# Seven of 32 convolution tasks moved from TensorE to GpSimd and VectorE, plain v spread in row halves, the last output tile in column halves, and a new order of all tasks

## The chip, the cores and the metric

One core of one Trainium2 chip runs one program. The metric is the device time of one execution in microseconds (us). The engines are TensorE (PE; its weight loads are listed as PEld), VectorE (DVE), ScalarE (ACT), GpSimd (POOL) and SyncE (SP), which issues nearly all DMAs.

## What is computed

Eight batches of eight heads of attention with a band mask, 576 positions of 64 features; the first four heads look at the 32 last positions (plain), the other four at every fourth of the last 128 (dilated). The result x is gated: a causal convolution over 5 positions per feature gives the gate, a matrix product the value, and a second product the output.

```python
scores = scale * np.matmul(q, k.transpose(0, 1, 3, 2))
mask_plain = (rel >= 0) & (rel < window)                # window 32
mask_dil = (rel >= 0) & (rel < window * dilation) & (rel % dilation == 0)   # dilation 4
scores = np.where(masks[None, :, :, :], scores, -1000000000.0)
attn = np.exp(scores - np.max(scores, axis=-1, keepdims=True))
attn = attn / (np.sum(attn, axis=-1, keepdims=True) + 1e-09)
attn_out = np.matmul(attn, v)
...
for k in range(K):                                      # K = 5
    gate_pre += conv_w[k][None, None, :] * xp[:, k:k + S, :]
gate = 1.0 / (1.0 + np.exp(-gate_pre))
out = (gate * (x @ w_val)) @ w_out
```

q, k, v are (8, 8, 576, 64), the weights 512x512 and 5x512, the output (8, 576, 512), all float32.

## The kernel before

The kernel is a list of some 820 tasks. A task is a function that emits a few instructions, an engine (or a choice of engines) with a cost, the tasks it depends on, and the buffers (`Ten`) that it uses. Buffers belong to classes with fixed counts (`TUNE["n"]`): `ps2` is three pairs of PSUM banks, `ps1` two single banks, `qk`, `va`, `vb`, `vp` hold loaded inputs, `et` exponentials, `xT` the attention result of a batch with features on the partitions, `gate` the gates, `osb` output tiles. `ORDER` is a written list of task numbers, each with a letter for its engine; `Plan.follow` (from line 550 on) emits them in that order, so each engine's queue is in the order of this list, and SP's DMAs too. A task waits for its dependencies and for the last user of the buffer that it is given. A load also waits until the bytes issued ahead of it are few enough (`ahead`). The planner's costs only choose which buffer of a class a task gets.

Names of tasks, with the batch as first digit:
- `Lq`, `Lk` with `p` or `d`: loads of q and k of the plain or dilated heads; `Lf`, `Lr`, `Lv`: plain v; `La`, `Lb`: dilated v; `Lwv`, `Lwo`: the weights, in buffers of class `va`.
- `Td`, `TKp`, `TQp` (L1071, L977): transposes of q and k, evicted by `Q..`, `K..` on ACT or DVE (L908, L910).
- `Sp`, `Sd` (L1001, L1113): scores; `Ep`, `Ed` (L931): exponentials on ACT; `Mp`, `Md`: masks, by two selects on POOL (L814, L816) or one multiplication on DVE (L942).
- `V1`, `V2` (L912): casts of dilated v on POOL; `H`: a clear of padding rows on POOL (L964).
- `Ap` (L1014), `Ad` (L1127, L1136): products with v; `Np`, `Nd`: normalisation on DVE; `Xp`, `Xd`: transposes into `xT`, evicted by `EXp`, `EXd`.
- `Pv` (L871, L877): for batches 0 and 1 plain v is loaded in whole rows and spread over the partitions by products with a 0/1 matrix `spread`, evicted by `Ev`.
- `C` (L1189): the convolution; `G` (L1199): tanh on ACT; `V` (L1207): the value product; `Y` (L1217): (gate + 1) times value on DVE. The digits are batch, half of the positions (288 each), half of the features.
- `O` (L1234): 36 output tiles of 128 positions; `EO` (L1242 on ACT, L1244 on DVE): their eviction; `ST` (L1248): the store.

The convolution on TensorE multiplies with diagonal matrices: for each of 5 taps, two feature chunks and two row halves one 64x64 matmul over 288 columns, 20 in all, four at a time in the four 64x64 quarters of the array. TensorE works in shapes (`mode`): 128 whole rows, `r64` two row halves, `c64` two column halves, `64` four quarters; neighbouring tasks of different shape change it. A value product depends on its convolution task (`t_c`), though it does not read it.

Of the kernel before, what the change touches and what calls it, by code (L numbers as in the profile page):

```python
# [8 lines left out]
FP32 = mybir.dt.float32  # L9
# [230 lines left out]
 'ahead': 7.06,  # L240
# [49 lines left out]
 'n': {'vf': 4,  # L290
# [4 lines left out]
       'va': 4,  # L295
       'vb': 3,
       'vab': 2,
       'vbb': 2,
       'qTp': 2,
       'kTp': 1,  # L300
       'qTd': 3,
       'kTd': 3,
       'et': 13,
       'xn': 5,
       'gate': 7,
       'osb': 15,
       'avt': 2,
       'xT': 3,
# [4 lines left out]
30s 2g 11d 8d 29s 9d 67s 118s 16a 0g 4a 3g 6d 1d 7d 5g 66s 40p 42p 10d 15g 41a 43a 14g 119s 12g  # L313
36p 38p 39d 37a 17a 55p 48p 68s 44p 49a 56a 59p 45a 69s 74p 31s 60a 46d 75d 76a 77p 32s 127p 79a
125p 126d 78a 95p 91p 33s 128d 131p 96a 57d 84p 156s 129p 85a 80p 130d 92a 155s 70p 50d 132a 93g
157s 86d 81a 13d 61d 137p 133p 34g 82d 72p 134a 97d 71a 35g 47p 158s 73d 51p 138a 121s 18p 52d
144p 122s 62p 145a 120s 58p 148p 63d 163p 149a 208s 53p 19a 164d 87p 165a 20g 83p 98p 64p 88d 166p
65a 23s 21s 94p 54a 161p 150d 207s 99d 168a 124g 167a 180p 135d 162d 184p 181a 173p 89p 123g 245s
174a 159p 139d 185a 146d 186d 244s 151p 160a 90d 147p 100p 152d 136p 140p 24g 101a 169p 218p 141d
170a 220p 106p 219a 171d 22g 102p 107a 175d 114p 103a 221d 153p 293s 292s 176p 115a 182d 172p 216p  # L320
108p 177d 217a 154a 214p 27s 109d 187p 183p 215a 116p 188d 226p 142p 25s 227a 117d 178p 246s 233p
222p 143d 234a 248p 223a 179d 251p 250d 249a 189p 104p 252d 253a 265p 105d 110p 266a 190d 258p
111a 254p 267d 299p 329s 303p 259a 199p 304d 255a 28g 260g 195p 235d 200a 191p 228d 196a 193p 256g
26d 300d 112p 192a 194d 330s 305p 113d 197p 306a 301p 198d 717p 247g 209s 211s 269p 718a 237p 210s
257p 261p 238a 732p 262d 270a 331s 203p 733a 271g 224d 336p 204a 302d 333p 239d 337a 322p 335d
723p 323a 338d 212g 415s 334a 272p 268p 729p 724a 273d 213g 225p 263p 730a 229p 343p 230d 339p
726p 340a 264d 344a 240p 414s 727d 307p 354p 308a 231p 236p 274p 355a 241d 205p 332g 378s 275a
294s 341g 201p 206d 232a 345d 276p 295s 356g 202d 296s 346p 277a 342p 242p 347d 738p 377s 243a
350p 311p 309d 318p 351a 720p 739d 319a 416s 352d 421p 312a 324d 418p 423a 422d 388p 420a 353p
297g 357p 278p 358d 419a 499s 298g 721a 288p 279d 428p 289a 359p 389d 280p 429a 360d 435p 281a  # L330
424p 430g 384p 390p 436a 385d 290p 313d 391a 437g 348p 425a 463s 291d 310p 314p 386p 315d 282p
387a 349d 379s 417g 439p 407p 320d 381s 440a 735p 500s 283d 408a 321p 316p 441d 736a 325p 462s
392p 317a 326d 396p 747p 393a 409d 380s 442p 397a 327p 748d 464s 438p 361p 328a 394d 362a 741p
465s 443d 403p 284p 404a 426d 365p 466s 742d 285a 369p 398d 366a 431p 370a 427p 473p 432d 503p
551s 506p 548s 504a 383g 505d 373p 507a 722s 382g 501s 471p 374a 286p 472d 508a 405d 469p 287d
474a 395p 399p 520p 400d 513p 750p 514a 470d 521a 410p 751d 524p 547s 509p 525a 401p 406p 433p
402a 411d 371p 526g 510a 475p 372d 375p 476a 467g 434a 481p 636s 376d 477p 482a 632s 412p 558p
413d 367p 478a 559a 483d 502g 585s 560p 368d 488p 584s 561a 468g 492p 753p 522d 493a 515g 479d
444p 586s 754a 523p 527p 445d 363p 489a 511g 528d 556p 480p 484p 557a 364d 446p 490d 450p 447a
485d 744p 451a 494d 491p 756p 745a 554p 495p 555a 454p 496d 458p 455a 757d 562p 497p 563a 516p  # L340
758s 486p 498d 634s 512p 459a 588p 725s 517d 591p 589a 759p 593a 487d 550s 587g 456p 592d 752s
746s 518p 457d 633s 460p 519a 670s 637g 760d 549s 743s 590a 762p 755s 461d 553g 573p 763d 598p
594p 595a 780p 599a 596g 669s 529p 452p 781a 574a 448p 600g 453d 749s 530a 564d 768p 449d 765p
769a 770s 609p 766d 566p 605p 764s 567a 771p 740s 782s 606a 641p 767s 772d 535p 610a 607g 635s
539p 536a 611d 531p 642d 540a 552g 575d 543p 532a 568d 577p 643p 578a 671s 537p 544a 579d 761s
608p 644a 612p 538d 533p 613d 645p 601p 597p 646a 777p 602d 778a 565p 639p 569p 534d 640a 673p
570d 676p 674a 783p 675a 677d 678a 576p 571p 784d 580p 731s 572a 662p 734s 581d 679p 728s 614p
680a 774p 719s 663a 785s 681d 672g 658p 615d 683p 638g 541p 684a 659a 685d 582p 545p 542d 583a
775a 660d 647p 690p 546d 648a 603p 786p 691a 604d 661p 787d 788s 692g 694p 651p 695a 792p 664d
652a 696d 665p 620p 666d 616p 621a 649d 628p 617a 653d 624p 793d 795p 625a 794s 629a 686p 682p  # L350
789p 796a 687d 697p 693p 630p 698d 667p 654p 631d 668a 626p 790d 650p 688p 655d 699p 689a 622p
# [51 lines left out]
class Plan:  # L403
# [86 lines left out]
    def emit(self, t, eng):  # L490
        t.ins = t.fn(eng)
# [878 lines left out]
```

## Time and profile before

| What | us |
|---|---|
| median of 3 runs | 167.81 (167.54 to 167.93) |
| the profiled execution | 168.98 |
| its span, first to last instruction | 167.3 |
| TensorE busy in it | 152.9 |
| convolution matmuls (L1189), busy | 23.0 |
| value products (L1207), busy | 35.8 |
| output products (L1234), busy | 34.1 |
| DMA, share of 16 engines over the span | 84.7% |

The profile is one execution. Busy time is the time in which an engine had an instruction under way; matmuls overlap, so a busy TensorE is not one at its peak. Rows of the groups name the line, the engine, the operation, what it writes and reads, the shape, the count, then busy time and mean duration, then idle time before and what ended it. The share of DMA over 100% in a stretch comes from packets that overlap.

### The profile page before, as it was taken

Reading aid. Unit: us, or ns where it says so; the run is one execution under the profiler, and the core shown is the slowest. Engines: PE = TensorE matmul, PEld = TensorE weight load, DVE = VectorE, ACT = ScalarE, POOL = GpSimd, SP = SyncE. Lnnn points to the kernel's source line nnn. Section 1 sums busy time; section 2 is a strip of 40 time slices with the busy share of each in tenths; the row PEclk is TensorE's granted clock in tenths of the full one; section 3 lists DMA queues with packets and bytes.
Section 4 is the critical chain, followed back from the end, with each engine's and each line's share of the span. In section 5 each row is a group of like instructions: output and inputs, shape, how many; then the busy total and the mean of one; then the engine's idle time right before and its main releaser. Section 6 shows DMA issues by size and latency. Waiting matters only on the chain.

```text
span 167.3 us, 6119 instructions
## 1 busy us (share of the span) xinstructions
PE 152.9 (91%) x2602; PEld 112.2 (67%) x2621; DVE 117.7 (70%) x250; ACT 110.1 (66%) x184; POOL 51.4 (31%) x86
## 2 busy tenths in 40 slices
PE   0898889989999999999997999999999999999991
PEld 0556677878776676786674876866687667785740
DVE  6127699989797888868757697784789787870520
ACT  4669567876847767777765885656686886357142
POOL 7802554430373370370030770009240221000000
PEclk9999999999999999999999999999999999999999
DMA  5999949999999999989999998179999902100995
GB/s 174 394 386 249 331 139 330 303 396 353 214 293 292 216 387 275 220 314 326 291 266 206 307 341 131 64 243 362 371 402 261 352 20 84 46 0 30 348 352 215
DMA packets 39442, 42.99 MB, mean 257 GB/s; under 512 B 20339, under 2 KB 27640, under 8 KB 39416
## 3 DMA queue, kind: packets, MB, share of 16 engines
q1 hardware_dynamic: 39376, 42.61, 84.7%
q8 instruction: 20, 0.33, 0.9%
q14 instruction: 6, 0.05, 0.1%
q10 hardware_dynamic: 40, 0.01, 0.0%
HBM read 33.17 MB, written 9.44 MB: 255 GB/s over the span
## 4 chain that ended last, share of the span: by engine, by line
PE 71%; DMA 15%; DVE 4%; SPq 4%; issue 2%; ACT 1%; POOL 0%; DVEq 0%; POOLq 0%
PE pd L1207 19%; PE pu L1234 18%; PE pd L1189 12%; DMA qk<-in_q_dram 8%; DMA vb<-in_v_dram 4%; PE pu L1071 3%; PE pd L1113 3%; PE pd L1014 3%; PE pd L1001 2%; PE pd L977 2%; DMA qk<-in_k_dram 2%; PE pu L1034 2%; PE pd L1127 2%; PE pu L1161 2%; SPq L899 2%
## 5 line engine op out<-in xcount | busy, mean ns | idle before, releaser
L931 ACT ACTIVATE et<-pd 128x576 bf16<-128x576 f32 x64 | 39.1, 652 | 13.8 <-PE pd L1113 6.5
L1207 PE MATMUL pd<-xT,w_val 128*128 128x288 bf16 x256 | 35.8, 286 | 0.3 <-DVE qTp L910 0.3
L1234 PE MATMUL pu<-w_out,ya 128*128 128x512 bf16 x126 | 34.1, 380 | 1.5 <-issue 0.8
L1217 DVE SCALAR_TENSOR_TENSOR ya<-gate,pd 128x576 bf16<-128x576 bf16 x32 | 23.7, 749 | 8.0 <-PE pd L1207 5.7
L1207 PEld LDWEIGHTS <-w_val 128*128 128x128 bf16 x256 | 23.7, 98 | 6.5 <-issue 0.6
L1199 ACT ACTIVATE gate<-pd 128x576 bf16<-128x576 f32 x32 | 20.3, 650 | 8.8 <-PE pd L1189 7.3
L1189 PE MATMUL pd<-xT,conv_diag 64*64 64x288 bf16 x640 | 23.0, 285 | 0.4 <-issue 0.2
L942 DVE TENSOR_TENSOR et<-et,mask_d 128x576 bf16<-128x576 bf16 x32 | 18.4, 586 | 3.1 <-ACT et L931 3.1
L814 POOL TENSOR_SCALAR_AFFINE_SELECT et<-et 128x576 bf16<-128x576 bf16 x15 | 11.6, 775 | 28.8 <-ACT et L931 25.6
L1234 PEld LDWEIGHTS <-ya 128*128 128x128 bf16 x144 | 12.2, 97 | 12.1 <-issue 0.9
L1189 PEld LDWEIGHTS <-conv_diag 64*64 64x64 bf16 x640 | 17.6, 106 | 3.4 <-issue 1.4
L1242 ACT ACTIVATE osb<-pu 128x512 f32<-128x512 f32 x21 | 12.6, 600 | 10.6 <-PE pu L1234 10.5
L1071 PE MATMUL pu<-perm_q,qk 128*128 128x128 bf16 x144 | 13.4, 231 | 5.2 <-DMA qk<-in_k_dram 4.7
L1025 DVE TENSOR_TENSOR xn<-pd,rec 96x768 bf16<-96x768 f32 x16 | 15.3, 954 | 0.7 <-DVE rec L1024 0.2
L908 ACT COPY xT<-pu 128x576 bf16<-128x576 bf16 x19 | 11.9, 644 | 5.7 <-PE pu L1161 2.8
L1071 PEld LDWEIGHTS <-qk 128*128 128x128 bf16 x144 | 9.9, 104 | 7.7 <-DMA qk<-in_k_dram 4.7
L1244 DVE TENSOR_SCALAR osb<-pu 128x512 f32<-128x512 f32 x15 | 10.3, 687 | 6.3 <-PE pu L1234 5.7
L1149 DVE TENSOR_TENSOR xn<-pd,rec 128x640 bf16<-128x640 f32 x16 | 13.2, 824 | 0.5
L912 POOL CAST vab<-va 128x1024 bf16<-128x1024 f32 x8 | 8.8, 1106 | 15.3 <-DMA va<-in_v_dram 15.3
L908 ACT COPY kTd<-pu 128x512 bf16<-128x512 bf16 (+1 forms) x12 | 9.0, 747 | 5.1 <-PE pu L1071 3.9
L816 POOL TENSOR_SCALAR_AFFINE_SELECT et<-et 128x576 bf16<-128x576 bf16 x15 | 11.5, 767 | 1.0
L942 DVE TENSOR_TENSOR et<-et,mask_p 128x576 bf16<-128x576 bf16 x17 | 10.0, 598 | 1.3 <-ACT et L931 1.2
(83 smaller groups left out, 209.1 us busy)
## 6 DMA issues: line engine op xcount, KB each, us to landing
qk<-in_k_dram SPq DMA_DIRECT2D x16, 576.0 KB, 6.8
qk<-in_q_dram SPq DMA_DIRECT2D x16, 576.0 KB, 6.7
out_dram<-osb SPq DMA_DIRECT2D x36, 256.0 KB, 3.5
va<-in_v_dram SPq DMA_DIRECT2D x10, 512.0 KB, 6.8
vp<-in_v_dram SPq DMA_DIRECT2D x6, 768.0 KB, 9.6
vb<-in_v_dram SPq DMA_DIRECT2D x16, 128.0 KB, 6.1
va<-in_moe_w_out_dram SPq DMA_DIRECT2D x6, 128.0 KB, 6.0
va<-in_moe_w_val_dram SPq DMA_DIRECT2D x2, 256.0 KB, 6.3
```

The costliest lines, as they stand in the source:

```text
L908: nc.scalar.copy(out=out_, in_=in_)
L931: nc.scalar.activation(out=view(), in_=ps2[ps.idx][:, :, 0:HW], func=AF.Exp, scale=scale)
L942: nc.vector.tensor_tensor(out=ev, in0=ev, in1=m, op=ALU.mult)
L1025: nc.vector.tensor_tensor(out=xn[xt.idx][0:96].rearrange("p (h j) l d -> p h (j l) d", h=2), in0=a[:, :, :, 0:D], in1=rr[:, :, :, None].to ...
L1071: nc.tensor.transpose(out=ov[:, e], in_=a[:, i * 128:(i + 1) * 128], identity=perm_q[o])
L1149: nc.vector.tensor_tensor(out=xn[xt.idx][:, 0:5].rearrange("p n x d -> p x n d"), in0=a[:, :, :, 0:D], in1=rr[:, :, :, None].to_broadcast( ...
L1189: nc.tensor.matmul(out=ps2[pc.idx][64 * ob:64 * ob + 64, n, 0:HW], lhsT=conv_diag[rb, 2 * cp + n, kk, :], rhs=xT[xt.idx][rb, 2 * cp + n, s ...
L1199: nc.scalar.activation(out=gate[g.idx], in_=ps2[pc.idx][:, :, 0:HW], func=AF.Tanh, scale=0.5)
L1207: nc.tensor.matmul(out=ps2[pv.idx][:, n, 0:HW], lhsT=w_val[:, mc, c * 128:(c + 1) * 128], rhs=xT[xt.idx][:, mc, c0:c0 + HW], start=(mc == ...
L1217: nc.vector.scalar_tensor_tensor(out=ya[yt.idx][:, 2 * cp:2 * cp + 2, t0:t0 + HW], in0=gate[g.idx], scalar=1.0, in1=ps2[pv.idx][:, :, 0:HW ...
L1234: nc.tensor.matmul(out=ps1[po.idx], lhsT=ya[yt.idx][:, c, t0:t0 + 128], rhs=w_out[:, c, :], start=(c == 0), stop=(c == NCH - 1))
L1242: nc.scalar.activation(out=osb[ob.idx], in_=ps1[po.idx], func=AF.Copy, scale=0.5)
```

## The change

1. `POOLED` names seven convolution tasks: second half, first features of batches 1 to 6, and first half, first features of batch 7. They become `Cp`: each tap is a scaling of `xT` by a weight per partition into `tap`, in two chunks of 288, and an addition to `acc` (fp32, two buffers). In the order six run on POOL; batch 2's runs on DVE as one scaling and four multiply-adds per chunk. Their tanh `Gp` reads `acc` in three pieces, since the quarters' exchange of halves is done here. No PSUM pair is used. The weights are copied once more, as fp32 (`conv_wf`).
2. Plain v of batches 0 and 1 is spread in one task `Pv`: blocks 0, 1 and 3, 4 need one half of the loaded rows each and are done in pairs of row halves; 32 matmuls are still issued, 8 of them small.
3. The last output tile is done as two tasks of 256 columns, `O35` and `O36`, each with its eviction and store.
4. Score tasks that stand beside a convolution in TensorE's queue are done in quarters (`keys`, `share`), with twice the matmuls; eleven are.
5. `V` no longer depends on `t_c`. Buffer counts change, `ahead` goes from 7.06 to 8.77, and `ORDER` is another list; most tasks stand at another place in it. POOL's selects of masks go from 15 tasks to 16; a cast of w_out moves from POOL to ACT, and the copies that make `perm_m` and `perm_r` from POOL to DVE.

In the new order the pooled tasks stand in POOL's queue so: `Mp110 Cp110 Mp210 H2`, `H4 Cp310 V14 V24`, `V25 Cp410 Cp510 H6 V26 V16 Mp611`, `V17 Cp610 Cp700`. On DVE: `Qd40 Cp210 Y211 Y201`. TensorE ends with `C710 C701 C711 O29 O28 V711 O27 V700 V701 O30 V710 O32 O31 O34 O33 O36 O35`.

```diff
- 'ahead': 7.06,
+ 'ahead': 8.77,
- 'n': {'vf': 4,
+ 'n': {'vf': 5,
...
-       'va': 4,
+       'va': 3,
-       'vbb': 2,
-       'qTp': 2,
+       'vbb': 5,
+       'qTp': 4,
...
-       'qTd': 3,
-       'kTd': 3,
-       'et': 13,
-       'xn': 5,
+       'qTd': 4,
+       'kTd': 2,
+       'et': 10,
+       'xn': 4,
+       'acc': 2,
-       'osb': 15,
+       'osb': 13,
-       'xT': 3,
+       'xT': 2,
...
+    def share(self, tasks):
+
+        run = []
+        for t in tasks + [None]:
+            if t and (t.form or t.mode == "64"):
+                run.append(t)
+                continue
+            if any(not u.form for u in run):
+                for u in run:
+                    if u.form:
+                        u.mode = u.leaves = "64"
+                        u.count *= 2
+            run = []
...
+    POOLED = [(b, 1, 0) for b in range(1, B - 1)] + [(B - 1, 0, 0)]
...
+    acc = tiles("acc", [128, 2, HW], FP32)
+    tap = consts.tile([128, 2, HW], FP32, name="tap")
...
+            def rows(j, rb, c, stop):
+                x0 = SP0 + R * (24 * j - 8) - c
+                nc.tensor.matmul(out=o[j // 4][:, j % 4], lhsT=spread[rb, x0:x0 + 128],
+                                 rhs=a[rb, :, c * D:(c + 1) * D], start=(c == 0), stop=stop)
+            for j in range(2):
+                for c in range(R):
+                    rows(j, slice(0, 64), c, c == R - 1)
+                    rows(j + 3, slice(64, 128), c, c == R - 1)
+            for j in (2, 5):
+                for c in range(R):
+                    rows(j, slice(0, 128), c, c == R - 1 and j == 2)
...
+    def keys(form):
+
+        parts = [slice(0, 128)] if form == "r64" else [slice(0, 64), slice(64, 128)]
+        return [(k, l) for k in parts for l in range(2)]
...
+                if (b, hf, cp) in POOLED:
+                    pc = Ten("acc")
+
+                def conv_p(eng, cp=cp, pc=pc, c0=c0, xt=xt):
+                    for kk in range(K):
+                        s0 = c0 + kk - (K - 1)
+                        for n in range(2):
+                            o = acc[pc.idx][:, n]
+                            i = xT[xt.idx][:, 2 * cp + n, s0:s0 + HW]
+                            w = conv_wf[:, 2 * cp + n, kk:kk + 1]
+                            if eng == DVE and kk:
+                                nc.vector.scalar_tensor_tensor(out=o, in0=i, scalar=w, in1=o, op0=ALU.mult, op1=ALU.add)
+                                continue
+                            e = nc.vector if eng == DVE else nc.gpsimd
+                            e.tensor_scalar(out=tap[:, n] if kk else o, in0=i, scalar1=w, scalar2=None, op0=ALU.mult)
+                        if eng == POOL and kk:
+                            nc.gpsimd.tensor_tensor(out=acc[pc.idx], in0=acc[pc.idx], in1=tap, op=ALU.add)
+
+                def th_p(eng, pc=pc, g=g):
+                    def go(o, i):
+                        nc.scalar.activation(out=o, in_=i, func=AF.Tanh, scale=0.5)
+                    go(gate[g.idx][:, 0], acc[pc.idx][:, 0])
+                    for hb in range(2):
+                        go(gate[g.idx][64 - 64 * hb:128 - 64 * hb, 1], acc[pc.idx][64 * hb:64 * hb + 64, 1])
...
+                if (b, hf, cp) in POOLED:
+                    t_c = plan.add(f"Cp{b}{hf}{cp}", {POOL: 9.0, DVE: 3.5}, conv_p, deps=dc, tens=[pc, g, xt], prio=p)
+                    t_g = plan.add(f"Gp{b}{hf}{cp}", {ACT: 1.05}, th_p, deps=[t_c], tens=[pc, g], prio=p)
...
-                               deps=[x_done[(b, c)] for c in range(NCH)] + w_ready["val"] + [t_c],
+                               deps=[x_done[(b, c)] for c in range(NCH)] + w_ready["val"],
...
+        for i, n0, n1 in [(i, 0, Dm) for i in range(last)] + [(last, 0, Dm // 2), (last + 1, Dm // 2, Dm)]:
+            t0 = 128 * min(i, last)
```

## The prediction

> **What bounds the kernel now.** I read the page's shares first, then the stretches, the chain that ended last, and the groups of the rows that the change prices.
>
> ```profile
> PE 152.9 (91%) x2602; PEld 112.2 (67%) x2621; DVE 117.7 (70%) x250; ACT 110.1 (66%) x184; POOL 51.4 (31%) x86
> PE 71%; DMA 15%; DVE 4%; SPq 4%; issue 2%; ACT 1%; POOL 0%; DVEq 0%; POOLq 0%
> ```
> ```profile
> 0.00:35.00 35.00, 27.74 (x492) 21.20 (x493) 23.27 (x89) 24.18 (x40) 16.96 (x38) 1.00 0.90 293
> 35.00:64.00 29.00, 28.38 (x510) 21.29 (x515) 24.09 (x40) 19.96 (x34) 11.73 (x17) 1.00 1.08 304
> 122.00:150.00 28.00, 27.68 (x491) 20.95 (x490) 23.16 (x41) 18.38 (x31) 3.50 (x5) 1.00 0.53 163
> ```
> The columns are the stretch, its length, busy us of PE, weight loads, DVE, ACT, POOL, then granted clock, DMA share, GB/s. From 35 us on TensorE is busy 28.4 of 29 and 27.7 of 28 us at full clock: there it sets the time, and POOL has room (3.5 of 28 us near the end). Before 35 us the loads set it, as the chain shows:
>
> ```profile
> 12.17 7.38 DMA vb<-in_v_dram
> ...
> 28.43 6.64 DMA qk<-in_q_dram
> ...
> 42.70 0.74 PE pd L1189 x20
> ...
> 120.28 2.58 PE pd L1189 x80
> ...
> 159.91 3.85 PE pu L1234 x17
> 163.78 0.60 ACT osb L1242
> ```
> (start, us, what.) The head is two DMA landings; a convolution task (20 matmuls of L1189) costs the path 0.74 us alone and 2.58/4 = 0.645 us in a run of four; the end is output matmuls, one eviction and a store.
>
> **The convolutions.** Seven of 32 tasks leave TensorE: 7 x 0.645 = 4.5 us off the path (0.74 each would be 5.2). I take 4.5, since most stood in runs. The order has 114 changes of tile shape between neighbouring tasks where it had 111; a change costs about 0.74 - 0.645 = 0.1 us, so +0.3. Eleven score tasks now take the 64x64 shape with twice the matmuls, 12 or 16 in place of 6 or 8; they save a change and double the issue, and I set both to nothing (bounds -1 to +1 us).
>
> **What a convolution costs where it goes.** Six go to POOL, one (batch 2) to DVE. Each POOL task is 10 scalings of 128x288 and 4 additions of 128x576 in fp32. The trace has neither; the nearest rows:
>
> ```profile
> L912 POOL CAST vab<-va 128x1024 bf16<-128x1024 f32 x8 | 8.8, 1106 | 15.3 <-DMA va<-in_v_dram 15.3
> L912 POOL CAST w_val<-va 128x256 bf16<-128x256 f32 x8 | 3.3, 459 | 2.8 <-DMA va<-in_moe_w_val_dram 2.8
> L1284 POOL TENSOR_TENSOR conv_diag<-ident,conv_w 128x1280 bf16<-128x1280 bf16 x1 | 2.3, 2329 | 2.7 <-ACT conv_w L908 2.7
> ```
> The undisturbed casts take 1.04 us for 1024 elements and 0.40 for 256, so 0.83 ns an element and 0.19 us to start: 0.43 us a scaling. An addition by the conv_diag row: 0.19 + 576 x (2329-190)/1280 ns = 1.15 us. With about 0.07 us at each dependent step (the gap between the two POOL selects of one mask), a task is 10 x 0.43 + 4 x 1.15 + 0.4 = 9.3 us. From below: additions at the casts' rate, 0.67 us, give 7.4. From above: fp32 moves twice the bytes of conv_diag's bf16, so twice its rate, 2.1 us, gives 13.1. I take 9.3, because conv_diag is also an operation on two tensors.
>
> The Trainium skill ("GPSIMD Engine Reference", Elementwise — side-by-side cycle accounting) gives 4497 ns for a two-input fp32 addition of 2048 elements; scaled, that estimates 1.26 us here and 9.7 us a task, 0.4 above mine. No run yet shows it.
>
> Beside that comes contention, seen in these lines (start, us, engine):
> ```profile
> 96.88 0.45 DVE L942 TENSOR_TENSOR et<-et,mask_d 128x576 bf16<-128x576 bf16 x1
> ```
> ```profile
> 96.97 0.93 POOL L816 TENSOR_SCALAR_AFFINE_SELECT et<-et 128x576 bf16<-128x576 bf16 x1
> 97.85 0.70 POOL L814 TENSOR_SCALAR_AFFINE_SELECT et<-et 128x576 bf16<-128x576 bf16 x1
> ```
> ```profile
> 98.07 0.79 DVE L942 TENSOR_TENSOR et<-et,mask_p 128x576 bf16<-128x576 bf16 x1
> ```
> The mask multiplication takes 0.45 us; the select that starts during it takes 0.93 in place of 0.71, and the multiplication that starts during the next select takes 0.79. The 49 multiplications range from 441 to 1286 ns. One waits for the other. With 48 multiplications in about 150 us some three meet each 9.3 us task, adding up to 3 x 0.45 = 1.3 us to it.
>
> The Trainium skill ("SBUF — State Buffer", SBUF: two separate sides) says the two engines' common port pair is an exclusive lock held for a whole instruction; the lines agree (0.79 against 0.45 us), and the rule speaks against putting fp32 work on POOL beside these masks.
>
> **Whether POOL keeps up.** I laid out the changed order of TensorE tasks by the mean distance in the trace between one task's first weight load and the next's (convolution 0.70, value product 0.99, output 0.79, scores 0.22 and 0.27 us, and so on), and POOL's queue beside it, at a round 9.0 us a convolution. Behind the convolutions wait clears, casts and masks that TensorE needs. Spare time: 0.7 us at Ap200 (clear H2 behind Cp110), 1.5 at Ad400 (cast V14 behind Cp310), 1.4 at Ap611 (mask behind Cp510). The last two tasks, Cp610 and Cp700, stand back to back after the cast V17 at 131.2; output O32 at 152.9 needs Cp700's tanh and product (1.2 + 0.75 us, and latency) and so the convolution by 150.8: twice its length may be 19.6 us. At 10.6 us for the masked ones and 9.3 for the last, the stalls are 0.9 + 0.1 + 0.2 + 0.3 = 1.5; at 9.3 about 0.3. I take 0.7 (bounds 0 to the slower rival's).
>
> **The DVE task** is 2 scalings and 8 multiply-adds of 128x288. The mask row's 445 ns (576 in two-byte form) bounds one from near: 2 x 0.3 + 8 x 0.445 = 4.2 us; half that if it starts cheaply. It holds DVE between a query eviction and the products Y211, Y201, which free PSUM pairs; three pairs exist. By the layout TensorE needs the first back about 1.9 us before DVE can give it at worst, and other work covers most: +0.5 (0 to 4.2). The seven tanhs are split in three (ACT takes 650 ns for 576 elements and 600 for 512, so 0.2 + 288 x 0.78 ns = 0.42 us each): about 1.2 us for 0.65, on an engine that is 66% busy: nothing on the path. But each waits in ACT's queue for POOL with evictions behind it: Gp410 ahead of a key eviction of batch 6 (transposes done at 102.4, Cp410 at 101.3 to 102.6) and Gp610 ahead of the last xT evictions (141.4, Cp610 at 140.5 to 141.8). At 10.6 us that is 0.4 us at most, and TensorE has value products to do meanwhile, so 0; each us beyond would show.
>
> **Plain v, buffers, tail.** A spread now has 8 pairs of half-row products and 8 whole ones in place of 24. The first task's 16 whole products take 1.76 us from its first weight load to the next task's, 0.11 each, so 8 fewer save 0.9 us a batch, 1.8 in all. Both lie before 35 us, where the landings above decide; I take 0 (bounds -1.8 to +2). The loss bound is from three weight buffers `va` for four: the load of w_val waits for a POOL cast, and the query load whose landing ends at 35.07 stands behind it on SP. Later loads land 1.8 us (q of dilated batch 4, at 70.0) or more ahead of their first use; by then two convolutions, 1.3 us, are saved, so this stays covered, but only just. In the tail half an eviction goes (0.60 us to about 0.4): -0.2, with one store more on SP, 0.43 us, issued while TensorE runs.
>
> **Sum:** -4.5 + 0.3 + 0.7 + 0.5 - 0.2 = -3.2 us. The profiled execution took 168.98 us: 167.3 of span and 1.7 around it; it becomes 165.8, the span 164.1. It lies 1.2 over the median of the runs, so the forecast is 167.8 - 3.2 = 164.6 us.
>
> **Rivals.**
> - *Everything hides* (17%): no stalls, and the head shortens by 1.8. -4.5 - 1.8 + 0.3 - 0.2 = -6.2: 161.6. For: TensorE is busy 27.7 of the first 35 us; against: the two landings.
> - *DVE is the new wait* (16%): Cp210 holds the PSUM pairs back 1.9 us rather than 0.5, and the normalisation Nd30 queued behind it (0.22 + 0.82 us) comes as a second wait of 1.0. -3.2 + 1.4 + 1.0 = -0.8: 167.0. For: 18 of 32 dilated masks met POOL already; against: the longer waits of TensorE on DVE after 35 us are two, 1.2 and 0.3 us.
> - *Slower: POOL cannot keep up* (17%). If a convolution takes 11.5 us (additions at 1.7), the stalls are 1.8 + 1.0 + 1.1, and 2 x 11.5 - 19.6 = 3.4 at the end: 7.3 for my 0.7. 164.6 + 6.6 = 171.2. It decides from 10.8 us a task, where the stalls (1.1 + 0.3 + 0.4 + 2.0) reach the 3.9 that the rest saves. For: fp32, two inputs, the waits on masks; against: conv_diag's row, and that masks are over by about 140 us, so that the last task runs clear.
> - *Gain and stall cancel within 0.2%* (8%), about 10.7 us a task: 167.8.
>
> **How the numbers follow.** The forecast has 42%; its own range is 162.8 to 166.3. Faster by over 0.2% (what these runs can tell from no change): 42 + 17 + 16 = 75%; same 8%; slower 17%. From 161.4, below the best case, to 167.9 all but the slower case is held.
>
> **What would show it.** L1189 at 500 matmuls and near 18 us busy; POOL near 105 us busy, each convolution 9 to 10.6 us from its first scaling to its last addition; scalings near 0.43, additions near 1.15 us; mask multiplications longer on average than 0.53 us; no wait of TensorE over 1 us on POOL; the last POOL addition at least 3 us ahead of O32. Additions near 2 us, or a hole in TensorE before O32, would make the forecast wrong; so would a later first value product than 35.5 us.

## The result and the profile after

The changed kernel takes 212.12 us (median of 4 runs, 211.33 to 213.93) where the kernel before takes 167.68: ratio 1.267 (95% interval 1.258 to 1.275). The forecast was 164.6, in a range of 161.4 to 167.9. The profiled execution took 213.93 us, its span is 212.2, against 167.3 before. In some experiments below (e6, e14 and e15 most) disturbed runs were left out of the ratio but not out of the median, so the text gives differences of medians and, where the two tell otherwise, differences of the ratios beside them.

The page's first parts for the changed kernel, busy time of the engines, the slices of TensorE, GpSimd and the granted clock, and the chain that ended last:

```profile
PE 167.2 (79%) x2557; PEld 116.1 (55%) x2557; DVE 128.5 (61%) x263; ACT 113.8 (54%) x197; POOL 146.1 (69%) x168
...
PE   1788779999809998939969999299479998089383
...
POOL 8205917559996332799957799999933999999700
PEclk9999975899995999985997999969999999658969
...
POOL 50%; PE 29%; DVE 6%; ACT 5%; issue 4%; DMA 3%; POOLq 1%; SPq 0%; DVEq 0%; ACTq 0%
```

GpSimd went from 51.4 to 146.1 us of work and from 0% to 50% of the chain. TensorE is no longer full after 35 us: holes (0, 2, 3, 4) stand where GpSimd shows a run of nines or has just ended one, and after each hole but one (the 4) the granted clock drops. (The 3 near 92 us is a wait for VectorE, which comes below with e6.) Groups of GpSimd, and TensorE's convolutions, on the page (busy us, mean ns of one, idle before):

```profile
L1229 POOL TENSOR_SCALAR tap<-xT,conv_wf 128x288 f32<-128x288 bf16 x48 | 50.2, 1056 | 1.8
...
L1231 POOL TENSOR_TENSOR acc<-acc,tap 128x576 f32<-128x576 f32 x24 | 34.8, 1452 | 2.0
...
L1247 PE MATMUL pd<-xT,conv_diag 64*64 64x288 bf16 x500 | 20.6, 307 | 7.1 <-ACT xT L934 6.8
```

A scaling takes 1.06 us where the prediction had 0.43, an addition 1.45 where it had 1.15. The timeline of GpSimd shows one whole task and what stands behind it (start us, us, and the instruction):

```profile
46.03 1.00 POOL L1229 TENSOR_SCALAR acc<-xT,conv_wf 128x288 f32<-128x288 bf16 x1 [1.94 <-DVE xT L936]
47.01 1.99 POOL L1229 TENSOR_SCALAR tap<-xT,conv_wf 128x288 f32<-128x288 bf16 x2
49.08 1.41 POOL L1231 TENSOR_TENSOR acc<-acc,tap 128x576 f32<-128x576 f32 x1
...
60.85 1.40 POOL L1231 TENSOR_TENSOR acc<-acc,tap 128x576 f32<-128x576 f32 x1
62.20 0.72 POOL L836 TENSOR_SCALAR_AFFINE_SELECT et<-et 128x576 bf16<-128x576 bf16 x1
62.98 0.71 POOL L838 TENSOR_SCALAR_AFFINE_SELECT et<-et 128x576 bf16<-128x576 bf16 x1
63.63 0.31 POOL L995 MEMSET vp<- 32x260 f32 x1
```

The task Cp110 runs from 43.1 to 62.3 (its second scaling, the first row above, waits 1.9 us for an xT eviction), and the clear of `vp` (H2), which the prediction named as first to be late, starts at 63.6. TensorE's timeline at the same place, and the stretches on either side (length, then busy us of PE, weight loads, DVE, ACT, POOL, granted clock, DMA share, GB/s):

```profile
63.99 0.82 PE L1046 MATMUL pd<-vp,et 128*128 128x65 bf16 x12 [6.38 <-POOL vp L995]
```
```profile
56.06:59.47 3.41, 1.55 (x36) 0.85 (x27) 2.40 (x3) 2.31 (x4) 3.23 (x4) 1.00 1.20 257
59.48:62.89 3.41, 0.00 (x0) 0.00 (x0) 0.00 (x0) 0.00 (x0) 3.33 (x4) 1.00 1.21 286
62.90:69.70 6.80, 5.71 (x71) 3.78 (x71) 2.70 (x4) 1.27 (x3) 3.89 (x7) 0.50 0.86 301
```

From 59.48 to 62.89 GpSimd is the only engine that works: everything waits for one clear of 0.3 us that is queued behind a convolution and a mask. Then TensorE runs two windows of 3.41 us at half clock. The view of waits, TensorE's own, shows the same trouble under other names:

```profile
PE pd L1046 <- POOL vp L995: 9.0, 2, 6.4
PE pd L1247 <- ACT xT L934: 6.8, 1, 6.8
...
PE pu L1297 <- DVE ya L1279: 4.1, 1, 4.1
```

(total us, times, longest.) The second and third do not name GpSimd, but lead to it: ScalarE's tanh waits for GpSimd's sum (20.7 us in all, by the view of every engine's waits), and the xT eviction and the product behind the tanh are late with it. That view's row of the tanh, and TensorE's timeline at the longest of these gaps:

```profile
ACT gate L1235 <- POOL acc L1231: 20.7, 4, 7.9
```
```profile
186.63 2.61 PE L1247 MATMUL pd<-xT,conv_diag 64*64 64x288 bf16 x40 [6.81 <-ACT xT L934]
```

TensorE has nine gaps of over a microsecond after 20 us, 31.7 us together, where the kernel before has one, of 1.17 us.

### The profile page after: what moved, and what is told of

It is laid out like the page before. It is cut to its first block, busy times and chain, and to the rows that moved or that the text cites. A ratio compares the mean times of both kernels' runs of the same rounds, so it can differ in the third digit from the quotient of the medians.

```text
span 212.2 us, 6125 instructions
## 1 busy us (share of the span) xinstructions
PE 167.2 (79%) x2557; PEld 116.1 (55%) x2557; DVE 128.5 (61%) x263; ACT 113.8 (54%) x197; POOL 146.1 (69%) x168
## 4 chain that ended last, share of the span: by engine, by line
POOL 50%; PE 29%; DVE 6%; ACT 5%; issue 4%; DMA 3%; POOLq 1%; SPq 0%; DVEq 0%; ACTq 0%
POOL tap L1229 24%; POOL acc L1231 15%; PE pu L1297 6%; POOL acc L1229 5%; PE pd L1269 4%; DMA qk<-in_k_dram 3%; PE pu L1103 3%; PE pd L1008 2%; DVE et L973 2%; PE pd L1247 2%; ACT et L962 2%; POOL vab L938 2%; POOL et L836 2%; POOL et L838 2%; PE pd L1046 2%
## 5 line engine op out<-in xcount | busy, mean ns | idle before, releaser
L1229 POOL TENSOR_SCALAR tap<-xT,conv_wf 128x288 f32<-128x288 bf16 x48 | 50.2, 1056 | 1.8
L1297 PE MATMUL pu<-w_out,ya 128*128 128x512 bf16 (+1 forms) x148 | 42.8, 424 | 4.2 <-DVE ya L1279 4.1
L1231 POOL TENSOR_TENSOR acc<-acc,tap 128x576 f32<-128x576 f32 x24 | 34.8, 1452 | 2.0
L836 POOL TENSOR_SCALAR_AFFINE_SELECT et<-et 128x576 bf16<-128x576 bf16 x16 | 11.7, 734 | 24.4 <-ACT et L962 24.4
L1297 PEld LDWEIGHTS <-ya 128*128 128x128 bf16 x148 | 13.8, 106 | 19.4 <-issue 7.0
L1235 ACT ACTIVATE gate<-acc 64x288 bf16<-64x288 f32 (+1 forms) x21 | 9.3, 441 | 20.9 <-POOL acc L1231 20.7
L1305 ACT ACTIVATE osb<-pu 128x512 f32<-128x512 f32 (+1 forms) x25 | 14.2, 580 | 10.4 <-PE pu L1297 10.2
L1255 ACT ACTIVATE gate<-pd 128x576 bf16<-128x576 f32 x25 | 15.8, 652 | 5.6 <-PE pd L1247 5.5
L1229 POOL TENSOR_SCALAR acc<-xT,conv_wf 128x288 f32<-128x288 bf16 x12 | 12.4, 1042 | 6.5 <-ACT xT L934 4.6
L1046 PEld LDWEIGHTS <-et 128*128 128x128 bf16 x192 | 8.5, 104 | 13.3 <-issue 10.2
L1046 PE MATMUL pd<-vp,et 128*128 128x65 bf16 x144 | 7.3, 206 | 10.4 <-POOL vp L995 9.0
```

Source lines behind the costliest of these rows:

```text
L836: nc.gpsimd.affine_select(out=dst, in_=dst, compare_op=ALU.is_ge, fill=0.0, base=base, pattern=pattern, channel_multiplier=-1)
L1046: nc.tensor.matmul(out=ps2[po.idx][:, hf, (2 * j + l) * DA:(2 * j + l + 1) * DA], lhsT=ex(e, l, 96 * j, 128), rhs=vv[:, 2 * l + x, 3 * hf ...
L1229: e.tensor_scalar(out=tap[:, n] if kk else o, in0=i, scalar1=w, scalar2=None, op0=ALU.mult)
L1231: nc.gpsimd.tensor_tensor(out=acc[pc.idx], in0=acc[pc.idx], in1=tap, op=ALU.add)
L1255: nc.scalar.activation(out=gate[g.idx], in_=ps2[pc.idx][:, :, 0:HW], func=AF.Tanh, scale=0.5)
L1297: nc.tensor.matmul(out=ps1[po.idx][:, 0:n1 - n0], lhsT=ya[yt.idx][:, c, t0:t0 + 128], rhs=w_out[:, c, n0:n1], start=(c == 0), stop=(c == N ...
```

## The experiments

Seventeen kernels, in four groups. Behind each expectation stand the kernel's median and its ratio to the kernel before, run on the same chip, with the 95% interval.

### How long GpSimd's convolution is

**e1: three taps of five.** `for kk in range(K if eng == DVE else 3):` in the convolution; two taps are left out on GpSimd.

> The changed kernel, but the six convolutions on GpSimd compute only the last-but... first three of their five taps (the other two are left out); nothing else is touched. By the rows of the changed kernel's profile such a task takes 2 x 1.00 + 2 x (2.0 + 1.5) = 9.1 us, which is the length that the prediction had priced (9.3). Theory A (the length of a convolution on GpSimd is the one mis-sized term): the rest of the sum holds and the time is about the forecast, 163 to 167 us. Theory B (the new order and the smaller buffers are slow in themselves, whatever GpSimd does): still over 175 us.

176.2 us, ratio 1.054 (1.045 to 1.063). A task takes 9.7 us from first to last instruction (median), and 36 of the 44 lost microseconds are gone. But theory A is out: with a task of about the length that was forecast the kernel is still 8.5 us slower than the one before.

**e2: one tap of five.** The same line with 1 for 3; four taps left out.

> The changed kernel with only the first of five taps on GpSimd (four taps are left out): 2.0 us a task, so that nothing can wait for GpSimd. Theory A: every stall on GpSimd is gone; 162 to 165 us, a little below the three-tap kernel. Theory B: no better than 168 us, because what is left is the order itself.

174.65 us, ratio 1.043 (1.035 to 1.051), at 2.3 us a task. So 7.4 us more in each of six tasks (2.3 to 9.7) cost 1.6 us in all: they are hidden, as the prediction's layout had it. What remains, 4%, isn't GpSimd's convolutions.

**e4: other forms of the same work, a single run.** Batch 3 scales by a constant, batch 4 scales 576 elements in one instruction, batch 5 writes two-byte results, batch 6 takes products of two tensors with the weight spread over the row (batch 3 has 0.25 for every weight, batch 4 the first half's weights for both).

```diff
+ if eng == POOL and b == 3: ... scalar1=0.25
+ if eng == POOL and b == 4: ... in0=xT[xt.idx][:, 2 * cp:2 * cp + 2, s0:s0 + HW], scalar1=conv_wf[:, 2 * cp, kk:kk + 1]
+ if eng == POOL and b == 5: ... out=(tapb if kk else accb)[:, n]
+ if eng == POOL and b == 6: nc.gpsimd.tensor_tensor(..., in1=conv_w[:, 2 * cp:2 * cp + 2, kk:kk + 1].to_broadcast([128, 2, HW]), op=ALU.mult)
```

> The changed kernel with a different form of the convolution in each batch on GpSimd, to price it (the results of batches 3 to 6 are not the convolution). Batch 1 and 7: as in the change, per-partition weight, 288 elements: 1.00 us each. Batch 3: the weight is an immediate. If reading the weight from memory is what costs, 0.43 us; if not, 1.0. Batch 4: one scaling over 576 elements in place of two over 288: 2.0 us if the cost is by the element (3.4 ns each), 1.2 if it is a start of 0.8 us. Batch 5: two-byte results: near 0.5 us if writing fp32 is what costs. Batch 6: the scaling as a multiplication of two tensors with the weight spread along 576, two-byte results: 1.2 to 1.4 us for both chunks, 2.0 if all arithmetic on GpSimd runs at 3.4 ns an element. Time of the whole: 195 to 212 us.

205.76 us. The groups of GpSimd in that run, by shape (the form of the change first, then two-byte results, the constant, 576 in one, and the product of two tensors):

```profile
L1261 POOL TENSOR_SCALAR tap<-xT,conv_wf 128x288 f32<-128x288 bf16 x16 | 16.7, 1056 | 0.6
...
L1238 POOL TENSOR_SCALAR tap<-xT,conv_wf 128x288 bf16<-128x288 bf16 x10 | 10.4, 1054 | 0.4
L1223 POOL TENSOR_SCALAR tap<-xT 128x288 f32<-128x288 bf16 x8 | 7.6, 964 | 0.3
L1230 POOL TENSOR_SCALAR tap<-xT,conv_wf 128x576 f32<-128x576 bf16 x4 | 6.9, 1725 | 0.3
L1245 POOL TENSOR_TENSOR tap<-xT,conv_w 128x576 bf16<-128x576 bf16 x5 | 6.0, 1201 | 0.2
```

Neither the weight's pointer (964 against 1056 ns), nor the four-byte result (1054), nor the instruction's start explains it: 576 elements cost 1725 ns and 288 cost 1000 undisturbed, so 2.5 ns an element and 0.28 us to start. The cast that the prediction scaled from moves an element in 0.83 ns. A product of two tensors is cheaper here than a product with one weight: 1201 ns for 576.

**e11: that form in all six tasks.** Taps as two-tensor products in two-byte type.

```diff
+ for kk in range(K if eng == POOL else 0):
+     nc.gpsimd.tensor_tensor(out=tapb if kk else accb, in0=xT[...], in1=conv_w[...].to_broadcast([128, 2, HW]), op=ALU.mult)
+     if kk:
+         nc.gpsimd.tensor_tensor(out=acc[pc.idx] if kk == K - 1 else accb, in0=accb, in1=tapb, op=ALU.add)
```

> The changed kernel with GpSimd's seven (six) convolutions in another form: each tap a product of two tensors in two-byte type, weights spread over the row, and sums in two-byte type but for the last. By the prices of the run on forms a task takes 11.9 us in place of 16.2. So a third dose between 9.1 us (176.2) and 16.2 us (212.1). Theory, margins of the layout are used up one after the other, and each stall is doubled by the clock: 180 to 187. Rival, cost goes straight with the length from the first us: 176.2 + (11.9 - 9.1) x 35.9 / 7.1 = 190.

192.72 us, ratio 1.153 (1.146 to 1.160), at 12.0 us a task: outside both. This form has a second price. VectorE's own convolution runs beside it, and its groups in e11 and in the change are:

```profile
L1235 DVE SCALAR_TENSOR_TENSOR acc<-xT,conv_wf,acc 128x288 f32<-128x288 bf16 x8 | 9.9, 1309 | 0.0
```
```profile
L1226 DVE SCALAR_TENSOR_TENSOR acc<-xT,conv_wf,acc 128x288 f32<-128x288 bf16 x8 | 6.0, 816 | 0.0
```

The last five of the eight multiply-adds take 1.40 to 1.52 us in e11, where the mean of all is 0.82 in the change: about the length of GpSimd's products and sums, 1.24 and 1.36, which run at that time without a pause. TensorE's gap behind that task (ahead of Ad300) grows from 3.35 us to 7.3, so about 4 of e11's microseconds are this. VectorE's masks grow too, from 0.67 and 0.51 us on average (dilated, plain) to 0.81 and 1.01, and two of TensorE's gaps in e11, of 3.1 and 1.7 us, lie behind a run of such masks. So e11 is not a pure dose of GpSimd's length. The four doses (median length of a task, from the traces):

| GpSimd task | time | per us of six tasks |
|---|---|---|
| 2.3 us (e2) | 174.65 | |
| 9.7 us (e1) | 176.2 | 0.03 |
| 12.0 us (e11) | 192.72 | 1.2 (0.9 without the 4 us) |
| 17.1 us (the change) | 212.12 | 0.63 (0.76) |

The last column is the difference in time over six times the difference in length. From e1 to the change, which have the same form, it is 0.8. So the price has a knee: up to 9.7 us a task it is near nothing, and beyond it, from somewhere between 9.7 and 12 us if e11 is trusted, a microsecond more in a task costs most of a microsecond.

### The clock after the stalls

The changed kernel runs 13 windows of 3.41 us, 44 us, at half clock; ten of these microseconds lie in the head. Does the slow clock cost, or only the stall before it?

**e10: warm filler in ten stalls.** Matmuls of zeros, in the kernel's own way of warming TensorE, ahead of the tasks that wait.

```diff
+FILL = {'Sd101': 3, 'Pv1': 6, 'Ap200': 24, 'Ad300': 12, 'Ad400': 5, 'Sp601': 13, 'Ap600': 9, 'Ap611': 5, 'C701': 25, 'O32': 15}
+            if t.name in FILL:
+                ...
+                self.constant(cls, i, FILL[t.name])
```

> The changed kernel as it is, with 117 matmuls of zeros put ahead of the ten tasks that its TensorE waits for longest (24 ahead of Ap200, 25 ahead of C701, 15 ahead of O32 and so on, each set about 0.8 of its gap long). Convolutions on GpSimd keep their 16.2 us. Theory, a good part of the 36 us that GpSimd costs is the half clock after each stall: the windows at 0.5 between 28.8 and 206 us vanish; TensorE was busy 11.3 of their 13 windows' worth, so at most 11.3 x 3.41 / 2 = 19 us: 195 to 202. Rival, GpSimd's queue sets the pace and TensorE only catches up with it: the windows vanish too, the stalls get longer by as much, and the time is 208 to 212.

213.5 us, ratio 1.277 (1.269 to 1.285), and no answer: two of the fillers needed a PSUM buffer that was itself held. They came behind their stall and took 5.5 and 8.4 us there.

**e16: without those two.** `FILL` without Sp601 and C701, Ad400 at 9.

> The run with filler in the stalls again, mended: there two fillers (ahead of Sp601 and C701) themselves waited for a PSUM buffer, came after the stall in place of during it, and held TensorE up by 5.5 and 8.4 us, so that run told nothing. Here these two are left out, and Ad400 has 9 in place of 5; 80 matmuls of zeros ahead of eight tasks. Theory, the half clock after stalls is a good part of GpSimd's price: the windows after 25 to 110 and at 203 us go, and 195 to 203 us. Rival, GpSimd sets the pace, and time that TensorE wins at full clock is waited away at the next task behind GpSimd: 207 to 212.

205.15 us, ratio 1.221 (1.215 to 1.227): 7 us less than the change. The granted clock and the chain of this run:

```profile
PEclk9999699999999999999999999889999999669969
...
POOL 55%; PE 19%; DMA 9%; ACT 6%; issue 4%; DVE 4%; POOLq 1%; SPq 1%; ACTq 0%; DVEq 0%
```

Five windows at half clock are left of 13. The first value product comes at 36.6 us, 4.2 earlier than in the change, and GpSimd's share of the chain rises from 50% to 55%. The gap ahead of C701, which has no filler now, is 6.8 us as before. So eight windows less, which could give 8 x 3.41 / 2 = 13.6 us at most, bought 7 of the 44 us, more than the rival allowed and less than the theory. What all 13 cost isn't shown; the pace is GpSimd's.

### The convolution on VectorE

**e6: e2 with Cp210 on GpSimd too** (its word in the order, `282d`, becomes `282g`; four taps left out of all seven).

> The one-tap kernel (four of five taps left out on GpSimd) with batch 2's convolution on GpSimd too, so that VectorE has none. In the one-tap kernel TensorE stands about 3 us around 80 to 90 us, where VectorE does its eight multiply-adds (816 ns each). If that task is the price, 170.5 to 172 us, 3 to 4 below the one-tap kernel; if the stall has another cause, 174 to 175.

171.32 us, ratio 1.010 (1.002 to 1.018): 3.3 us less than e2, or 5.5 by the ratios. The chain of e2 at that place (start, us, what):

```profile
76.42 0.48 DVE qTd L936
76.91 1.38 DVE acc L1229 x2
78.29 4.87 DVE acc L1226 x7
...
83.44 0.51 DVE acc L1226
83.94 0.68 DVE ya L1279
```
```profile
84.67 0.42 PE L1160 MATMUL pd<-vab,et 128*128 128x65 bf16 x8 [3.10 <-DVE ya L1279]
```

VectorE's task takes 7.1 us, the product Y behind it is late, and TensorE (second fence, its timeline) stands for 3.10 us. That is the wait that the prediction described and put at 0.5. In e6 TensorE has no such gap there.

### What the rest of the change costs

**e3: all seven convolutions back on TensorE.** `POOLED = []`, seven words of the order moved back ahead of their value products; no other part undone.

> The changed kernel with all seven convolutions back on TensorE as matmuls, each placed as late before its value product as the buffers allow; everything else of the change stays. Theory A: the rest of the change is worth about nothing, so 7 x 0.645 = 4.5 us above the one-tap kernel: 166 to 169 us, about the kernel before. Theory B: the order and the buffers cost by themselves: over 172 us.

175.2 us, ratio 1.046 (1.036 to 1.055). So the new order with its buffers, the spread, the score shapes and the tail cost 7.5 us before any convolution moves, and taking the seven out (e6, 171.32, with one tap of five on GpSimd) gives back 3.9, or 6.0 by the ratios.

**e12: the kernel before, four taps left out in the same seven tasks.** What TensorE can save at all:

```diff
-                    for kk in range(K):
+                    for kk in range(K - 1 if few else 0, K):
```

> The kernel before, with four of five taps left out in the same seven tasks (4 of 20 matmuls each); order, tasks and everything else as before. It prices what TensorE can save at all. The prediction's term, 7 x 0.645 us, would be here 0.8 x 4.5 = 3.6: 164.1 us, ratio 0.979. Rival, other engines hold TensorE as soon as it is quicker: 166.5 to 167.7.

165.33 us, ratio 0.987 (0.982 to 0.992): 2.45 us for four fifths, so an estimate of 3.1 for the seven whole tasks (1.7 to 3.8 by the interval), not 4.5.

Three runs then changed one part of the head of e3, whose first value product stands at 39.1 us (35.4 before).

**e5: four weight buffers.** `'va': 4` in e3.

> The kernel with all convolutions on TensorE again, but four buffers of class va as before the change in place of three (the room comes from acc and tap, which it does not use). It asks where the 4 us of its head come from (first value product at 39.1 us, 35.4 in the kernel before). Theory S (the loads of w_val wait for a buffer, SP's queue stands and everything after is late): the first value product comes 2 to 4 us earlier and the time falls to 171 to 173 us. Theory L (a mask on VectorE waits for conv_diag on GpSimd, TensorE stands and its clock falls): the first value product stays at 38 to 40 us, 174 to 176 us.

**e7: whole rows in the spread.** `for j in (0, 1, 3, 4, 2, 5)` with `slice(0, 128)` in e3: 24 whole products a batch in place of 16 half ones and 8 whole.

> The kernel with all convolutions on TensorE, and the spread of plain v done with whole rows again (24 products of 128 rows in place of 16 half ones and 8 whole), still one task. If the half rows run in pairs, as I had priced (0.9 us a batch), this is 0 to 2 us slower than with them: 175 to 177 us. If the halves do not overlap (the profile shows singles of 0.20 us), it is faster: 173 to 175, with the spread task 3.3 to 3.6 us in place of 4.0.

**e8: conv_diag built on VectorE** instead of GpSimd, in e3.

> The kernel with all convolutions on TensorE, and the one multiplication that builds conv_diag on VectorE in place of GpSimd, at the same place in the order. Theory L: the mask multiplication behind it takes 0.45 us in place of 1.8, but VectorE is busy 1.4 us itself; the first value product 0 to 1.5 us earlier, 173.5 to 175.5 us. Theory S: no change at all.

e5 takes 174.18 us (ratio 1.037, 1.029 to 1.045; first value product at 37.9), e7 178.19 (1.056, 1.045 to 1.067; 41.9) and e8 175.0 (1.039, 1.029 to 1.049; 37.5). None is the cause. Against e3 the buffer is worth about 1 us, and half rows look better than whole ones in this order (3.0 us, 1.7 by the ratios), though the intervals overlap in both cases. In e8 a first value product 1.6 us earlier buys nothing at the end.

**e9 and e17: warm filler in the head of e6.** Its granted clock, and two windows of it (columns as above), show why one would try:

```profile
PEclk9998765999999999999999999999999999999999
```
```profile
12.53:15.94 3.41, 1.97 (x38) 1.20 (x35) 2.85 (x13) 3.21 (x6) 0.00 (x0) 1.00 1.14 303
15.94:19.35 3.41, 3.06 (x36) 2.06 (x37) 2.14 (x14) 1.84 (x4) 1.19 (x1) 0.50 1.04 280
```

TensorE is busy for 1.97 of 3.41 us in the first, with no gap longer than 1.1 us, and the second comes at half clock.

```diff
+FILL = {'Sp011': 1, 'Td110': 1, 'Sd101': 4, 'Sd110': 2, 'Ap010': 5, 'Ad100': 3}
```

> The kernel with one tap in each of the seven tasks, all on GpSimd (four of five taps left out), and 16 matmuls of zeros by 128x512 put ahead of six tasks of the head that wait (Sp011 1, Td110 1, Sd101 4, Sd110 2, Ap010 5, Ad100 3). Nothing else moves. Without them: 171.3 us (median), with three windows of 3.41 us at a granted clock of 0.5 between 15.9 and 29.6 us, in which TensorE was busy 0.90, 0.64 and 1.00 of the time. Theory, the new order's head costs through the clock that its gaps bring: no such window, and at most (0.90 + 0.64 + 1.00) x 3.41 / 2 = 4.3 us less; 167.5 to 169. Rival, the head is late because its inputs come late: the windows may go, the time stays at 171 to 172, and the gaps get longer.

> The run with filler in the head again, without the two single matmuls ahead of Sp011 and Td110, of which the first waited 0.9 us for its own buffer. 14 left. If these two cost what they held up, 168.5 to 169 us against 169.4; if the head waits for its inputs anyway, 169.4 again. A half-clock window at 16 us may come back: then 171.

169.42 us (ratio 1.012, 1.007 to 1.017) and, without the first two entries, 169.44 us (1.011, 1.006 to 1.015). No window at half clock is left in the head of either. Against e6 it is 1.9 us less by the medians and nothing by the ratios, so whether the filler pays isn't shown. The first value product comes at 36.2 us in e17, against 39.3 in e6 and 34.2 in e12.

**e13: the old order and buffers with the new parts,** convolutions on TensorE.

> The order, the buffer counts and all 32 convolutions on TensorE of the kernel before, with the other parts of the change: v spread in row halves (one task a batch, put where the second of the old two stood), score tasks in the shape of their neighbours, the last output tile in column halves. Against the kernel with the new order and all convolutions on TensorE (175.2 us, ratio 1.046) it differs in order and buffers alone. Theory, the new order costs those 4.6% and the new parts nothing: 166 to 168.5, ratio 0.99 to 1.005, first value product at 34 to 36 us and no window at half clock before the end. Rival, the spread in row halves brings the late head: first value product at 38 to 39 us, ratio 1.02 or more.

170.81 us, ratio 1.020 (1.013 to 1.026). The head is back: first value product at 34.6 us, no half clock. The order with its buffers is thus 4.4 us of e3's 7.5, but not all. What in the order makes the head 4.5 us late stays open: e5, e7 and e8 don't find it. This trace also has a hole of 2.4 us inside one transpose task at 86 us, for which the profile shows no releaser ("issue"); why isn't known.

**e14: e13 with score tasks in their own shape.** The call of `share` is taken out, 60 matmuls fewer.

> The kernel of the run before this one (old order and buffers, all convolutions on TensorE, spread in row halves, last tile in column halves), with one thing taken out: score tasks keep their own shape of 64x128 and are not doubled to 64x64 where they stand beside one; 60 matmuls fewer. In that run's trace all Sp tasks hold TensorE 8.0 us, against 6.3 in the kernel before with fewer taps, Sd 7.0 in both. Theory, the doubling costs 1.7 us that the prediction set to nothing: 169 us, ratio 1.010. Rival, it is free: 170.8, ratio 1.020, and what is left lies in the tail and in a gap at 86 us.

**e15: the kernel before with the spread in row halves,** and no other part of the change.

> The kernel before with nothing changed but the spread of v in row halves: two tasks of 32 matmuls in place of four of 16. The two hold TensorE 5.2 us against 6.9 for the four, by the traces of the last run and of the kernel before with fewer taps. Theory: 1.7 us less, 166 us, ratio 0.990: the one part of the change that pays. Rival, the halves come later (one task waits for both loads and for two PSUM buffers), and the head waits for the mask instead: 167.5 to 168.5, ratio 1.000 to 1.006.

e14 takes 169.42 us (ratio 1.009, 1.005 to 1.013) and e15 169.11 (1.006, 1.001 to 1.011). Without the doubled score matmuls the kernel is 1.4 us quicker (1.9 by the ratios). That the doubling costs this is likely but not clean, since e14's trace also lacks the hole of 2.4 us at 86 us (it has one of 0.8 at 89). The half rows take TensorE 5.2 us for the two batches, 6.9 before, and yet the kernel isn't quicker with them but slightly slower: one task now depends on both loads and both PSUM buffers and stands later (Pv0 from 16.5, where Pv00 ran from 14.8 in e12). In e15's timeline TensorE stands 1.45 us for a key eviction until 16.0, at a place that Pv00 fills in e12. The tail in column halves is left with 0.3 us, which these runs can't tell from nothing.

## Why the prediction was wrong

From the kernel before to the change, in steps:

| step | median | difference | by the ratios |
|---|---|---|---|
| before | 167.7 | | |
| order, buffers, spread, score shapes, tail (e3) | 175.2 | +7.5 | +7.6 |
| seven convolutions off TensorE (e6) | 171.3 | -3.9 | -6.0 |
| one of them on VectorE (e2) | 174.65 | +3.3 | +5.5 |
| GpSimd's task from 2.3 to 9.7 us (e1) | 176.2 | +1.6 | +1.8 |
| to 17.1 us (the change) | 212.1 | +35.9 | +35.8 |

**The step that failed: "10 x 0.43 + 4 x 1.15 + 0.4 = 9.3 us".** An undisturbed task (Cp700) takes 16.1 us: ten scalings of 1.00, four additions of 1.40, and 0.5 between them. Six tenths of a microsecond too little in each scaling makes 5.7 of the 6.8 us. The price came from the casts, as one more operation with one input. The bounds, 7.4 to 13.1, were drawn on the addition alone; the scaling had one kind of row behind it and no upper end, though it comes ten times and the addition four. Another one-input row of that trace, the selects with 0.71 us for 576 elements, lies near the casts' rate (0.67) and gave no warning. With twice the casts' rate as a bound for the scaling too, the upper end would have been 15.5, far inside the slower rival.

**A second step failed without GpSimd: the order was no term of the sum.** With a task of 9.7 us, about the length forecast, e1 takes 176.2 us, 8 us above the upper end of the range. The sum had +0.3 for changes of tile shape, nothing for the doubled scores and the spread, and up to +2 for the head, where e3 measures +7.5 for all of these with the new order and its buffers.

**The mechanism was right, as the rival had it.** "POOL cannot keep up" named the clear behind Cp110, the cast behind Cp310, the mask behind Cp510 and the end, free up to about 9 to 10 us a task. The runs agree (9.7 us costs 1.6 us). Its own arithmetic at 16.1 us gives 6.4 + 5.6 + 5.7 + 12.6 = 30.3 us of stalls; of the nine gaps, the seven behind GpSimd make 26.6 us. (The other two are Pv1 in the head, 1.8, and Ad300 behind VectorE, 3.35.) The total agrees better than its parts. The clear costs 6.38 us as computed, but the cast 1.53 for 5.6, the clear and the mask behind Cp510 4.05 for 5.7, and the end 10.9 for 12.6. At two places that the prediction named in ScalarE's queue and put at nothing ("so 0; each us beyond would show") it did show: a key eviction behind the tanh Gp410, 3.7 us, which the arithmetic leaves out, and the last xT evictions behind Gp610, 6.8 us, which are most of the end. At 12.0 us it gives 2.3 us for the clear, and e11 has 2.4 there; e11's other gaps are mixed with VectorE's masks and don't test it.

**The clock was not in the sum.** Seven of the nine gaps are followed by windows at 0.5; the gaps at 152.8 and 155.8 us are not. TensorE's busy time rose from 152.9 to 167.2 us with about as many matmuls. How much of that lies on the path isn't shown in full; by e16, eight of the 13 windows are worth some 7 us of the 44.

**The convolutions, -4.5:** an estimate of -3.1 in the old order (e12), and -3.9 in the new (-6.0 by the ratios). In the old order the chain's 0.645 us a task is what the task occupies, not what its removal frees; the new order doesn't decide it.

**The VectorE task, +0.5 (0 to 4.2):** +3.3, inside the bounds, or +5.5 by the ratios, outside. Mis-sized was the task, 7.1 us for 4.2: a multiply-add of 288 elements took 0.82 us (0.50 to 1.28), not 0.445.

**The small parts.** The doubled scores, set "both to nothing (bounds -1 to +1 us)", look like +1.4 (1.9 by the ratios), outside the bounds, with e13's hole as a doubt. "Plain v ... I take 0 (bounds -1.8 to +2)": +1.2 alone in the old order, inside the bounds, though TensorE does save 1.7 us there. For the head the text asked for a first value product by 35.5 us and allowed +2 for the buffers. It came at 40.8 in the change and at 39.1 in e3; the order with its buffers does it (34.6 in e13), and what in the order isn't known. Of its 4.4 us warm filler buys back between nothing and 1.9.

**Contention** was about right: up to 1.3 us a task was expected. Without their waits for xT the five others take 16.6 to 17.3 us, where the last, alone, takes 16.1.

## What to carry to other kernels

Work moved to an idle engine is free only until it holds up the small instructions queued behind it: lay out that margin (here about 10 us a task), and then price the moved operation with bounds on each of its parts, the most numerous first, since past the knee most of every microsecond was paid. Price the removal of a task from a busy engine below its duration (an estimate of 0.4 us for 0.645 here, in the old order), and undo the parts one at a time: here the convolutions' removal from TensorE paid, and neither the new order nor the half-row spread did, though the spread does shorten its engine's work.

## What the runs showed of the hardware

- **GpSimd, product with one weight:** 2.5 ns an element and 0.28 us to start (288: 1.00, 576: 1.72), and about the same with a constant for the weight (0.96) or a two-byte result (0.99); a cast 0.83 ns an element, a product of two bf16 tensors 1.20 us for 576, a sum of two fp32 tensors 1.40 us for 576.
- **Clock:** grants change in steps of 3.41 us, and a window of TensorE at 58% busy, no gap over 1.1 us, was followed by one at half clock (e6). The busy share alone does not decide: in the change, windows at 45, 55 and 47% (from 56.1, 148.2 and 151.6 us) were followed by full clock. The Trainium skill ("TensorE: Matmul & The Clock Gate", Part 1) gives this window, 3413 ns and free-running, and the traces agree (boundaries at 62.90 us in the change and at 15.94 in e6 lie 13.8 windows apart, so the grid does not start with the kernel); it ties the drop to an idle window, where these traces show it after one that was busy for more than half.
- **VectorE beside GpSimd:** a mask on VectorE that takes 0.45 us alone took 2.58 beside a GpSimd operation of 2.60, in the change. The Trainium skill ("SBUF — State Buffer", SBUF: two separate sides) calls the port pair a lock held for a whole instruction, and these two timeline rows agree, as do e11's multiply-adds of 1.40 to 1.52 us:

```profile
23.99 2.58 DVE L973 TENSOR_TENSOR et<-et,mask_d 128x576 bf16<-128x576 bf16 x1
```
```profile
23.66 2.60 POOL L1349 TENSOR_TENSOR conv_diag<-ident,conv_w 128x1280 bf16<-128x1280 bf16 x1
```
- **VectorE:** a multiply-add of 288 elements with a weight per row took 0.50 to 1.28 us, 0.82 on average, and a scaling 0.77 (both in the change, some of them beside GpSimd's work), where a mask's product of 576 two-byte elements takes 0.45.
